# Moving the float64 pieces back by two units, and the packed product's low part forward by one, in a fused attention and MLP kernel

## Chip, cores and metric

The kernel runs on one core of one Trainium2 chip. The metric is device microseconds of one execution. Three runs of the kernel before gave 1552.0, 1552.22 and 1557.69 us, median 1552.22.

## What is computed

The reference, cut to what matters (8 batches, 8 heads, 576 tokens, head size 64, 32 packing queries; 4608 tokens of 512 features go through two MLPs with 1536 and 2048 hidden features):

```
def sm_attn(qq, kk, vv):
    s = scale * np.matmul(qq, kk.transpose(0, 1, 3, 2))
    s = s - np.max(s, axis=-1, keepdims=True)
    a = np.exp(s)
    a = a / (np.sum(a, axis=-1, keepdims=True) + 1e-09)
    return np.matmul(a, vv)
p_packed = sm_attn(p, k, v)
x = sm_attn(q, p_packed, p_packed)          # heads joined to 4608 x 512
x = ((x @ moe_w_a) * (x @ moe_w_b)) @ moe_w_out
h = x @ moe2_w_in
out = (h * np.clip(h + 3.0, 0.0, 6.0) / 6.0) @ moe2_w_out
```

The weights of the MLPs come from the host as float64 words.

## The kernel before

Engines: PE multiplies matrices, PEld loads its weights, DVE, ACT and POOL work on vectors, SP issues the DMAs. Each engine and SP's queue take their instructions in the order in which the program emits them; nothing reorders them later, so the order of the Python calls is the schedule.

Matrices in float32 are multiplied as a high and a low part: `mm3` (L58 to L61) issues three matmuls, high by high, and each high by the other's low. ACT makes a high part by a cast, and DVE or POOL the low part as a difference.

The first MLP is done in four groups of two batches (1152 tokens), each in 12 steps of 128 hidden features: steps 0 to 47, step t belongs to group t // 12. The last matrix of attention, the packed values, is multiplied into the first MLP's weights first. So a step has these parts:

- `pw_unit(t + 1)` (L395): the packed product for the next step, 32 small matmuls (L409) into two of the three PSUM banks named `att`. ACT casts both banks to `pw_hi` (L411). DVE then makes `pw_lo` (L415), which is the last reader of the banks. This subtraction isn't emitted at once: `later(2, rest)` puts it on a list, and `tick()` (L123), called behind each unit of a step and each `y_unit`, counts down and emits what is due.
- four `ab_unit`s (L422), each 12 matmuls of 288 columns, six into each of two tiles in the three `ab` banks. ACT copies the first tile to `a` (L435), DVE multiplies it by the second to `g` (L437), ACT casts `g_hi` (L443), POOL makes `g_lo` (L444).
- `y_unit`s (L452): nine matmuls into one of two `y` banks, then a sum into `acc` on DVE (L464), in the first quarter of a group a copy on ACT (L462). There are 16 for every three steps, emitted between the units as they become ready: in the third step of three, behind the third `ab` unit, first.

The five units of a step come in the order `ab`, `pw`, `ab`, `ab`, `ab`. Behind each unit two slots are filled with background work:

- attention for the next group (`att_units`), whose scores (L176, the tiles `s`) also need two `att` banks at a time,
- in group four, preparation of the second MLP's weights (`w_prep`),
- in groups one to three, **pieces**: 128 x 512 float64 words are rounded to float32. `piece_units` gives five parts for each: two ACT passes (L81, L82) and a DVE shift (L84); a second DVE pass (L88); the store of the piece before (L372); a third DVE pass (L93), which needs ACT's square; POOL's sum (L96), after which the next load is issued. Group one converts the first MLP's weights, groups two and three the second's: 32 pieces, one in a step or two in each third step. Group four has none.

`parts` in the main loop (L711) puts the parts of a step's pieces into slots, two to a unit. In groups two and three they are spread over the first six slots of a step, which begin behind the first `ab` unit, before the packed product.

Behind the first MLP (from about 778 us) the second runs, in six token tiles by eight weight products, with three weight matmuls each as well.

Of the kernel before, what the change touches and what calls it, by code (L numbers as in the profile page):

```python
# [23 lines left out]
NM1 = F1 // P  # L24
# [16 lines left out]
def f32(ap):  # L41
    return ap.bitcast(F32)
# [3 lines left out]
def tile_kernel(ctx: ExitStack, tc: tile.TileContext, qT, kT, vn, pT, wab, wo1, win, wo2, out):  # L46
# [73 lines left out]
    def later(n, fn):  # L120
        due.append([n, fn])
# [19 lines left out]
    def bank(name):  # L141
        tag = banks[n_bank[0] % len(banks)]
        n_bank[0] += 1
        return psum.tile([P, 512], F32, tag=tag, name=name, bufs=BANKS[tag])
# [3 lines left out]
    def lhs_tiles(g):  # L148
        lhs[g] = main.tile([P, 2, 4, NP], F32, tag="lhs", name=f"lhs{g}", bufs=2)
# [130 lines left out]
    def at_split(b, cs=(0, 1)):  # L280
        if b not in at_t:
            at_t[b] = (
                main.tile([P, 2, S], F32R, tag="at_hi", name=f"at_hi{b}", bufs=3),
                main.tile([P, 2, S], F32R, tag="at_lo", name=f"at_lo{b}", bufs=3),
            )
        hi, lo = at_t[b]
        for c in cs:
            a = at32_t.pop((b, c))
            act.copy(hi[:, c, :], a)

            (dve if b == 1 and c == 0 else pool).tensor_sub(lo[:, c, :], a, f32(hi[:, c, :]))  # L291
# [7 lines left out]
    def att_units(b):  # L299

        pk, sf = pack_units(b), soft_units(b)
        lq = [lambda j=j: load_kq(qT, "q", b, j) for j in range(2)]
        ld = loads(b + 1)
        return lq[:1] + pk[:2] + lq[1:] + pk[2:] + ld[:3] + sf[:2] + ld[3:] + sf[2:]
# [13 lines left out]
    def wab_load(t):  # L318

        if NM1 <= t < NSTEP:  # L320
            sp.dma_start(rab_tile(t), wabf[t % NM1])

    def wo_load(t):
        if NM1 <= t < NSTEP:
            m = t % NM1
            sp.dma_start(ro_tile(t), wo1f[m * P:(m + 1) * P, :])
# [68 lines left out]
    def pw_unit(t, wait=2):  # L395

        if t >= NSTEP:
            return
        l = lhs[t // NM1]
        w = rab_t[t].rearrange("p (q n) -> p q n", q=4)  # L400
        hi = main.tile([P, 2, 2, 256], F32R, tag="pw_hi", name=f"pw_hi{t}", bufs=2)
        lo = main.tile([P, 2, 2, 256], F32R, tag="pw_lo", name=f"pw_lo{t}", bufs=2)
        pw_t[t] = (hi, lo)
        ps = [bank(f"pw{t}_{c}").rearrange("p (b n) -> p b n", b=2) for c in range(2)]
        for b in range(2):
            for q in range(4):
                for c in range(2):
                    r, o = slice(64 * c, 64 * c + 64), slice(NP * q, NP * q + NP)
                    pe.matmul(ps[c][o, b, :], lhsT=l[r, b, q, :], rhs=w[r, q, :], start=True, stop=True)  # L409
        for c in range(2):  # L410
            act.copy(hi[:, c], ps[c])  # L411

        def rest():
            for c in range(2):
                dve.tensor_sub(lo[:, c], ps[c], f32(hi[:, c]))  # L415

        if wait:
            later(wait, rest)
        else:
            rest()  # L420
# [112 lines left out]
    def wo_prep(rpool, p):  # L533

        z = {}

        def load():
            z["r"] = rpool.tile([P, 2, CP], F32, tag="raw", name=f"raw_wo{p}")
            for i in range(2):
                sp.dma_start(z["r"][:, i], p2f[2 * p + i, 1])  # L540

        def parts(opool, i):
            hi = opool.tile([P, DM], F32R, tag=f"wo2_hi{p}{i}", name=f"wo2_hi{2 * p + i}")
            lo = opool.tile([P, DM], F32R, tag=f"wo2_lo{p}{i}", name=f"wo2_lo{2 * p + i}")
            wo2_t[2 * p + i] = (hi, lo)
            act.copy(hi, z["r"][:, i])
            pool.tensor_sub(lo, z["r"][:, i], f32(hi))

        return load, parts

    def y_units(pool_, tt):

        z = {}

        def load():
            z["r"] = pool_.tile([P, 4, TP], F32, tag="raw", name=f"raw_y{tt}")
            for k in range(4):
                sp.dma_start(z["r"][:, k], y1d[k, :, tt * TP:(tt + 1) * TP])

        def blk(n):  # L560
            k, j = int(n[1]) - 1, int(n[2]) - 1
            return z["r"][:, 2 * k:2 * k + 2, j * TH:(j + 1) * TH]

        def get(n):
            return blk(n) if n[0] == "B" else z[n]

        def add(to, a, b):
            def fn():
                z[to] = pool_.tile([P, 2, TH], F32, tag="ty", name=f"ty{tt}_{to}", bufs=3)
                pool.tensor_sub(z[to], get(a), get(b))  # L570
            return fn

        def part(n):
            def fn():
                hi = pool_.tile([P, 2, TH], F32R, tag=f"yh{n}", name=f"yh{tt}_{n}")
                lo = pool_.tile([P, 2, TH], F32R, tag=f"yl{n}", name=f"yl{tt}_{n}")
                y_t[n] = (hi, lo)
                act.copy(hi, get(n))
                (pool if n[0] == "B" else dve).tensor_sub(lo, get(n), f32(hi))
            return fn  # L580

        first = [add("T1", "B12", "B11"), add("T2", "B22", "T1"), add("T3", "B22", "B12")]
        t4 = add("T4", "B21", "T2")
        def part4():
            t4()
            part("T4")()
        return load, first, {1: part("B11"), 6: part("T2"), 2: part("B21"), 7: part("T3"), 5: part("T1"), 4: part4, 3: part("B22")}
# [5 lines left out]
    def spread(work, n):  # L593

        return [work[len(work) * i // n:len(work) * (i + 1) // n] for i in range(n)]
# [84 lines left out]
    for t in range(NSTEP):  # L680
        g, m = divmod(t, NM1)
        if m == 0 and g + 1 < NG:
            lhs_tiles(g + 1)
            b = 2 * g + 2
            u0, u1 = att_units(b), att_units(b + 1)
            bg = u0 + u1[:1] + [lambda b=b: at_split(b, (0,))] + u1[1:2] + [lambda b=b: at_split(b, (1,))] + u1[2:]
        if m == 0 and g + 1 == NG:
            sp.dma_start(*stores[-1])
            es_att.close()
            p2a = es_p2a.enter_context(tc.tile_pool(name="p2a", bufs=1, side="right", reuse_waits="tile"))  # L690
            y_load, y_first, y_part = y_units(p2a, 0)
            wo_load0, wo_parts0 = wo_prep(p2a, 0)
            bg = w_prep(p2a, list(range(1, NW)) + [0])
            bg += [y_load, lambda: None, lambda: None] + y_first + [y_part[k] for k in (1, 6, 2, 7, 5, 4, 3)] + [wo_load0]
        wo_load(t + 1)
        left = NM1 - 1 - m
        nb = len(bg) if left == 0 else -(-len(bg) // left)
        todo, bg = spread(bg[:nb], 10), bg[nb:]
        units = [
            (ab_unit, t, 0, 0),  # L700
            (pw_unit, t + 1),
            (ab_unit, t, 0, 1),
            (ab_unit, t, 1, 0),
            (ab_unit, t, 1, 1),
        ]

        if g == 0:
            n_conv = len(by_step[m])
        else:
            n_conv = 2 * NM2 * (t - NM1 + 1) // (2 * NM1) - 2 * NM2 * (t - NM1) // (2 * NM1) if g < 3 else 0  # L710
        parts = spread(list(range(5 * n_conv)), 9 if n_conv > 2 else 6 if g > 0 or n_conv == 2 else 3) + [[]] * 7  # L711
        now = []
        for i, (u, *x) in enumerate(units):
            if (u.__name__[:2], *x) not in ahead:
                u(*x)
            tick()
            if i == 1:
                wab_load(t + 3)
            if g == 0:

                for x in splits.get((t, i), ()):
                    wo_split(*x)
            elif m % SW < 2 and i in (1, 2):
                wo_split(t, i - 1)
            elif m % SW == 1 and i == 4:
                wo_split(t + 1, 0)
            elif m % SW == 2 and i == 1:
                wo_split(t, 1)
            if i in (3, 4) and m == NM1 - 1 and g + 1 < NG:
                at_split(2 * g + 3, (i - 3,))  # L730
            for k in range(2):
                for _ in parts[2 * i + k]:
                    if not now:
                        now = piece_units()
                    now.pop(0)()
                for fn in todo[2 * i + k]:
                    fn()
                if y_ready and (k == 0 or i in (1, 3)) and (y_ready[0][0] * NM1 + y_ready[0][1] * SW + SW - 1, y_ready[0][2] // 2) in wo_t:
                    y_unit(*y_ready.pop(0))
                    tick()  # L740
# [194 lines left out]
```

## Time and profile before

The profile is of one execution, which took 1552.25 us; its span, first to last instruction, is 1550.5 us.

| | PE | PEld | DVE | ACT | POOL |
|---|---|---|---|---|---|
| busy us | 1491.7 | 1347.3 | 872.3 | 682.0 | 491.9 |
| share of the span | 96% | 87% | 56% | 44% | 32% |

Busy is the union of an engine's instructions. Matmuls overlap: one of 288 columns is shown as 0.29 us long, and the next starts 0.13 us after it. Where a row ends in brackets, the number there is the idle time of the engine before it, and behind the arrow stands what ended it. The granted clock of PE is 1.0 of full speed from 150 us on.

### The profile page before, as it was taken

To read this page: it belongs to the slowest core of one execution; us is meant where nothing else is said; L and a number is where in the kernel's file an instruction comes from. 1 tells how busy PE (TensorE), PEld (TensorE's weight loads), DVE (VectorE), ACT (ScalarE), POOL (GpSimd) and SP (SyncE) were. 2 spreads that over 40 slices of the span, in tenths; PEclk is the share of its full clock that TensorE was granted. 3 is DMA by queue.
4 is the path that set the end of the run, shared out by engine and by line. 5 is a ranking of instruction groups with operands and counts; after the bars stand their busy time and mean duration, and the time that the engine had idled before them with its cause. 6 is when DMAs were issued, how large, how long until landed. Compare 5 with 4: busy or idle time off the path is not lost. (4 is left out here: it accounts for less than half of the span.)

```text
span 1550.5 us, 27991 instructions
## 1 busy us (share of the span) xinstructions
PE 1491.7 (96%) x11128; PEld 1347.3 (87%) x11128; DVE 872.3 (56%) x1592; ACT 682.0 (44%) x1453; POOL 491.9 (32%) x483
## 2 busy tenths in 40 slices
PE   4799999999999999999999999999999999999998
PEld 2588898888989899999989988998998998998997
DVE  5778784555754666545544464455455446455443
ACT  4566554554555545554423343343343334234332
POOL 2576653453634545554711130030020021011000
PEclk9799999999999999999999999999999999999999
DMA  8775555655466433664354334344344344333331
GB/s 288 218 220 177 184 191 176 194 160 179 124 198 188 138 125 106 235 219 170 120 180 178 129 141 178 116 162 149 130 152 167 107 172 143 136 144 133 142 138 41
DMA packets 75954, 250.06 MB, mean 161 GB/s; under 512 B 7856, under 2 KB 26288, under 8 KB 68784
## 3 DMA queue, kind: packets, MB, share of 16 engines
q1 hardware_dynamic: 75824, 248.28, 46.6%
q8 instruction: 87, 1.43, 0.4%
q14 instruction: 43, 0.35, 0.1%
HBM read 196.87 MB, written 51.38 MB: 160 GB/s over the span
## 5 line engine op out<-in xcount | busy, mean ns | idle before, releaser
L59 PE MATMUL ab<-at_hi,pw_hi 128*128 128x288 f32 x768 | 234.0, 305 | 8.3 <-ACT a L435 5.5
L61 PE MATMUL ab<-at_hi,pw_lo 128*128 128x288 f32 x768 | 229.1, 298 | 4.3 <-DVE pw_lo L415 4.3
L59 PE MATMUL y<-g_hi,wo_hi 128*128 128x288 f32 x768 | 231.3, 301 | 1.8 <-DVE acc L464 1.7
L60 PE MATMUL ab<-at_lo,pw_hi 128*128 128x288 f32 x768 | 228.6, 298 | 1.2 <-POOL at_lo L291 0.6
L61 PE MATMUL y<-g_hi,wo_lo 128*128 128x288 f32 x768 | 226.4, 295 | 1.0 <-POOL wo_lo L393 1.0
L60 PE MATMUL y<-g_lo,wo_hi 128*128 128x288 f32 x768 | 226.9, 295 | 0.4 <-POOL g_lo L444 0.4
L60 PE MATMUL o<-wo_lo,g2h 128*128 128x512 f32 x576 | 225.0, 391 | 0.0
L61 PE MATMUL o<-wo_hi,g2l 128*128 128x512 f32 x576 | 224.9, 390 | 0.0
L59 PE MATMUL o<-wo_hi,g2h 128*128 128x512 f32 x576 | 224.7, 390 | 0.0
L444 POOL TENSOR_TENSOR g_lo<-g,g_hi 128x288 fp32r<-128x288 f32 x192 | 164.4, 859 | 176.8 <-ACT g_hi L443 172.4
L783 DVE TENSOR_TENSOR g2l<-u,g2h 128x384 fp32r<-128x384 f32 x192 | 121.7, 634 | 140.9 <-ACT g2h L782 136.0
L437 DVE TENSOR_TENSOR g<-a,ab 128x288 f32<-128x288 f32 x192 | 86.4, 451 | 171.7 <-PE ab L61 112.3
L59 PEld LDWEIGHTS ab<-at_hi,pw_hi 128*128 128x128 f32 x768 | 146.6, 191 | 23.7 <-ACT a L435 7.6
L59 PEld LDWEIGHTS y<-g_hi,wo_hi 128*128 128x128 f32 x768 | 144.2, 188 | 19.4 <-DVE acc L464 9.1
L774 ACT ACTIVATE r<-c,half_b 128x384 f32<-128x384 f32 x144 | 88.9, 617 | 144.4 <-DVE c L767 143.9
L61 PEld LDWEIGHTS ab<-at_hi,pw_lo 128*128 128x128 f32 x768 | 146.3, 191 | 4.6 <-DVE pw_lo L415 4.5
L60 PEld LDWEIGHTS ab<-at_lo,pw_hi 128*128 128x128 f32 x768 | 146.5, 191 | 1.7 <-POOL at_lo L291 0.9
L570 POOL TENSOR_TENSOR ty_T<-raw_y 128x768 f32<-128x768 f32 x12 | 23.4, 1952 | 387.1 <-DMA raw_y<-y1d 387.1
L435 ACT COPY a<-ab 128x288 f32<-128x288 f32 x192 | 76.2, 400 | 157.9 <-PE ab L61 156.9
L61 PEld LDWEIGHTS y<-g_hi,wo_lo 128*128 128x128 f32 x768 | 144.3, 188 | 1.5 <-POOL wo_lo L393 1.5
L60 PEld LDWEIGHTS y<-g_lo,wo_hi 128*128 128x128 f32 x768 | 144.3, 188 | 0.6 <-POOL g_lo L444 0.6
L782 ACT CAST g2h<-u 128x384 fp32r<-128x384 f32 x192 | 98.7, 514 | 86.1 <-DVE u L776 84.7
(323 smaller groups left out, 3058.1 us busy)
## 6 DMA issues: line engine op xcount, KB each, us to landing
w<-w2d SPq DMA_DIRECT2D x47, 1792.0 KB, 7.3
rab<-wabf SPq DMA_DIRECT2D x36, 512.0 KB, 5.2
f64p<-in_wo SPq DMA_DIRECT2D x28, 512.0 KB, 3.7
w2d<-w SPq DMA_DIRECT2D x8, 1792.0 KB, 6.7
f64p<-in_wab SPq DMA_DIRECT2D x24, 512.0 KB, 4.6
k<-in_kT SPq DMA_DIRECT2D x16, 576.0 KB, 5.3
q<-in_qT SPq DMA_DIRECT2D x16, 576.0 KB, 5.2
ro<-wo1f SPq DMA_DIRECT2D x36, 256.0 KB, 3.7
```

Source lines behind the costliest of these rows:

```text
L59: pe.matmul(ps, lhsT=l_hi, rhs=r_hi, start=first, stop=False, skip_group_check=skip)
L60: pe.matmul(ps, lhsT=l_hi, rhs=r_lo, start=False, stop=False, skip_group_check=skip)
L61: pe.matmul(ps, lhsT=l_lo, rhs=r_hi, start=False, stop=last, skip_group_check=skip)
L435: act.copy(a, ps[0])
L437: dve.tensor_mul(g32, a, ps[1])
L444: pool.tensor_sub(gl, g32, f32(gh))
L570: pool.tensor_sub(z[to], get(a), get(b))
L774: act.activation(r, c, AF.Relu, bias=half_b, scale=1.0 / 6.0)
L782: act.copy(hi, u)
L783: dve.tensor_sub(lo, u, f32(hi))
```

## The change

Two edits. In `pw_unit` the low part of products for step 12 and later is put on the list with 1, not 2, so that it is emitted by the `tick()` directly behind the product. In the main loop, in groups two to four, four empty slots are put ahead of the pieces' parts: they begin behind the second `ab` unit.

```
-        if wait:
+        if wait and t >= NM1:
+
+            later(1, rest)
+        elif wait:
             later(wait, rest)
         else:
             rest()
...
         parts = spread(list(range(5 * n_conv)), 9 if n_conv > 2 else 6 if g > 0 or n_conv == 2 else 3) + [[]] * 7
+        if g > 0:
+
+            parts = [[]] * 4 + parts
```

PE's instructions stand in the same order before and after. On the other engines the order is another from step 11 on, and from there lines are numbered 3 higher. The first place is DVE in step 17, around the low part of the product for step 18. The names: `g_17_0` is the product for step 17's first `ab` unit, `cv_ap` a piece, `pw_lo` the low part. Before:

```order
L437 TENSOR_TENSOR g_17_0_4531<-a_0_4529,ab_01_4522 128x288
L84 TENSOR_SCALAR cv_ap_0_4541<-f64p_0_3905 128x512
L88 SCALAR_TENSOR_TENSOR cv_ap_0_4541<-f64p_0_3905,cv_ap_0_4541 128x512
L93 SCALAR_TENSOR_TENSOR cv_ap_0_4541<-cv_sqp_0_4538,cv_ap_0_4541 128x512
L84 TENSOR_SCALAR cv_ap_1_4585<-f64p_1_3943 128x512
L437 TENSOR_TENSOR g_17_1_4607<-a_1_4605,ab_11_4598 128x288
L415 TENSOR_TENSOR pw_lo_4548<-pw_0_4549,pw_hi_4547 128x512
L415 TENSOR_TENSOR pw_lo_4548<-pw_1_4550,pw_hi_4547 128x512
```

The same place in the changed kernel:

```order
L440 TENSOR_TENSOR g_17_0_4531<-a_0_4529,ab_01_4522 128x288
L415 TENSOR_TENSOR pw_lo_4540<-pw_0_4541,pw_hi_4539 128x512
L415 TENSOR_TENSOR pw_lo_4540<-pw_1_4542,pw_hi_4539 128x512
L440 TENSOR_TENSOR g_17_1_4591<-a_1_4589,ab_11_4582 128x288
L84 TENSOR_SCALAR cv_ap_0_4599<-f64p_0_3953 128x512
L88 SCALAR_TENSOR_TENSOR cv_ap_0_4599<-f64p_0_3953,cv_ap_0_4599 128x512
L440 TENSOR_TENSOR g_17_2_4633<-a_2_4631,ab_21_4624 128x288
L93 SCALAR_TENSOR_TENSOR cv_ap_0_4599<-cv_sqp_0_4596,cv_ap_0_4599 128x512
```

The low part has moved ahead of four passes of pieces and of `g_17_1`.

The second place is ACT in step 14, from the cast of the product for step 15 to the copy of the third `ab` unit. `cv_sqp` and `p2f` are a piece's two passes, `a_1` and `a_2` the copies of the second and third `ab` unit. Before:

```order
L81 ACTIVATE cv_sqp_0_3863<-f64p_0_2971 128x512
L82 ACTIVATE p2f_0_3862<-f64p_0_2971 128x512
L236 COPY lhs_3297<-bd_3870 128x128
L411 CAST pw_hi_3873<-pw_0_3875 128x512
L411 CAST pw_hi_3873<-pw_1_3876 128x512
L443 CAST g_hi_0_3858<-g_14_0_3856 128x288
L392 CAST wo_hi_3899<-ro_3555 128x256
L81 ACTIVATE cv_sqp_1_3908<-f64p_1_3176 128x512
L82 ACTIVATE p2f_1_3907<-f64p_1_3176 128x512
L435 COPY a_1_3929<-ab_10_3915 128x288
L435 COPY a_2_3959<-ab_20_3945 128x288
```

In the changed kernel:

```order
L236 COPY lhs_3297<-bd_3862 128x128
L411 CAST pw_hi_3865<-pw_0_3867 128x512
L411 CAST pw_hi_3865<-pw_1_3868 128x512
L446 CAST g_hi_0_3858<-g_14_0_3856 128x288
L392 CAST wo_hi_3893<-ro_3555 128x256
L438 COPY a_1_3913<-ab_10_3899 128x288
L81 ACTIVATE cv_sqp_0_3920<-f64p_0_2971 128x512
L82 ACTIVATE p2f_0_3919<-f64p_0_2971 128x512
L438 COPY a_2_3943<-ab_20_3929 128x288
```

The first piece has moved from before the product's cast to behind `a_1`, the second to a place after these rows.

The third place is POOL at the border of groups three and four. `p2f` are the sums of the last two pieces, `at_lo` is the attention output's low part, and `raw_w` the first weight sums of group four, which follow these rows. Before:

```order
L96 TENSOR_TENSOR p2f_0_8670<-cv_ap_0_8674,p2f_0_8670 128x512
L96 TENSOR_TENSOR p2f_1_8710<-cv_ap_1_8714,p2f_1_8710 128x512
L444 TENSOR_TENSOR g_lo_1_8735<-g_35_1_8732,g_hi_1_8734 128x288
L291 TENSOR_TENSOR at_lo_8765<-at_8607,at_hi_8764 128x576
L444 TENSOR_TENSOR g_lo_2_8761<-g_35_2_8758,g_hi_2_8760 128x288
L291 TENSOR_TENSOR at_lo_8765<-at_8644,at_hi_8764 128x576
L444 TENSOR_TENSOR g_lo_3_8813<-g_35_3_8810,g_hi_3_8812 128x288
L444 TENSOR_TENSOR g_lo_0_8856<-g_36_0_8853,g_hi_0_8855 128x288
```

In the changed kernel:

```order
L447 TENSOR_TENSOR g_lo_1_8721<-g_35_1_8718,g_hi_1_8720 128x288
L291 TENSOR_TENSOR at_lo_8753<-at_8605,at_hi_8752 128x576
L96 TENSOR_TENSOR p2f_0_8722<-cv_ap_0_8726,p2f_0_8722 128x512
L447 TENSOR_TENSOR g_lo_2_8749<-g_35_2_8746,g_hi_2_8748 128x288
L291 TENSOR_TENSOR at_lo_8753<-at_8644,at_hi_8752 128x576
L447 TENSOR_TENSOR g_lo_3_8809<-g_35_3_8806,g_hi_3_8808 128x288
L96 TENSOR_TENSOR p2f_1_8772<-cv_ap_1_8776,p2f_1_8772 128x512
L447 TENSOR_TENSOR g_lo_0_8856<-g_36_0_8853,g_hi_0_8855 128x288
```

The last piece's sum now stands behind all low parts of step 35; its store, and on SP's queue the loads for `raw_w` behind it, follow that sum.

## Rows read from the trace of the kernel before

**Rows 1.** The page, busy us by engine: share of the span, instructions.

```profile
PE 1491.7 (96%) x11128; PEld 1347.3 (87%) x11128; DVE 872.3 (56%) x1592; ACT 682.0 (44%) x1453; POOL 491.9 (32%) x483
```

**Rows 2.** Stretches: us, then busy PE, PEld, DVE, ACT, POOL; PEclk, DMA, GB/s.

```profile
224.00:612.00 388.00, 377.15 (x3819) 343.97 (x3825) 230.64 (x454) 198.06 (x471) 185.76 (x202) 1.00 0.49 156
612.00:778.00 166.00, 165.12 (x1489) 156.58 (x1480) 82.33 (x153) 81.58 (x195) 95.66 (x112) 1.00 0.53 187
```

**Rows 3.** Waits of PE, 224 to 612 us: us in total, times, longest us.

```profile
PE s L176 <- DVE pw_lo L415: 4.0, 3, 2.7
PE ab L59 <- ACT a L435: 3.5, 5, 0.7
PE y L59 <- DVE acc L464: 1.7, 2, 1.3
PE pv L226 <- ACT et L215: 0.6, 2, 0.3
PE y L60 <- POOL g_lo L444: 0.4, 1, 0.4
```

**Rows 4.** Waits of PE, 612 to 778 us.

```profile
PE ab L59 <- ACT a L435: 0.4, 1, 0.4
PE ab L59 <- DVE g L437: 0.4, 1, 0.4
```

**Rows 5.** Timeline of PE, a stopped and a free block: start us, us, instruction.

```profile
320.03 0.67 PE L176 MATMUL s<-k,p 64*32 64x288 f32 x2
323.38 0.71 PE L176 MATMUL s<-k,p 64*32 64x288 f32 x14 [2.69 <-DVE pw_lo L415]
324.03 0.40 PE L59 MATMUL ab<-at_hi,pw_hi 128*128 128x288 f32 x1
...
331.00 0.71 PE L176 MATMUL s<-k,p 64*32 64x288 f32 x16
331.65 0.40 PE L59 MATMUL ab<-at_hi,pw_hi 128*128 128x288 f32 x1
```

**Rows 6.** Timeline of ACT and DVE, step 17, ahead of that block.

```profile
318.40 1.07 ACT L411 CAST pw_hi<-pw 128x512 fp32r<-128x512 f32 x2
...
322.18 0.45 DVE L437 TENSOR_TENSOR g<-a,ab 128x288 f32<-128x288 f32 x1 [1.21 <-ACT a L435]
322.55 1.28 DVE L415 TENSOR_TENSOR pw_lo<-pw,pw_hi 128x512 fp32r<-128x512 f32 x2
```

**Rows 7.** Timeline of PE and ACT, step 14.

```profile
276.11 0.29 PE L61 MATMUL ab<-at_hi,pw_lo 128*128 128x288 f32 x1
277.12 0.40 PE L59 MATMUL ab<-at_hi,pw_hi 128*128 128x288 f32 x1 [0.72 <-ACT a L435]
...
275.24 0.42 ACT L392 CAST wo_hi<-ro 128x256 fp32r<-128x256 f32 x1
...
276.67 0.70 ACT L435 COPY a<-ab 128x288 f32<-128x288 f32 x2
```

**Rows 8.** Timeline of ACT and PE, group four, step 38, the same place.

```profile
644.14 0.41 ACT L435 COPY a<-ab 128x288 f32<-128x288 f32 x1
...
644.75 0.30 PE L61 MATMUL ab<-at_hi,pw_lo 128*128 128x288 f32 x1
644.88 0.29 PE L59 MATMUL ab<-at_hi,pw_hi 128*128 128x288 f32 x1
```

**Rows 9.** Timeline of POOL and DVE, two passes that overlap.

```profile
309.26 1.16 POOL L271 TENSOR_TENSOR t<-t,sm 128x576 f32<-128x576 f32 x1 [0.97 <-DVE sm L270]
...
309.45 1.51 DVE L93 SCALAR_TENSOR_TENSOR cv_ap<-cv_sqp,cv_ap 128x512 f32<-128x512 f32 x1
```

**Rows 10.** Groups by line, 224 to 612 us: count, busy us, mean ns, idle before.

```profile
L81 ACT ACTIVATE cv_sqp<-f64p 128x512 f32<-128x512 f32 x33 | 22.7, 688 | 0.0
...
L93 DVE SCALAR_TENSOR_TENSOR cv_ap<-cv_sqp,cv_ap 128x512 f32<-128x512 f32 x33 | 26.3, 798 | 0.9
```

**Rows 11.** Timeline of POOL, the first weight sum of group four.

```profile
617.84 0.73 POOL L509 TENSOR_TENSOR raw_w<-raw_w 128x256 f32<-128x256 f32 x1 [2.60 <-DMA raw_w<-p2f]
```

## What the change should do

> **What bounds the kernel now.** First the page's busy times: PE, the matrix engine, works 96% of the span of 1550.5 us, the next engine 56% [rows 1]. So time can come only out of PE's idle time, and it has to be looked for where the change acts. That is from 224 us, just before the packed product for the first step of group two is made, to the end of group four. The table by stretches [rows 2] cuts this at 612 us, in the first step of group four: up to there PE is busy 377.15 of 388.00 us, so 10.85 idle; after it 165.12 of 166.00, so 0.88. Then PE's waits in the first stretch, sorted by who ended them [rows 3]: 4.0 us for the packed product's low part (three times, once 2.7), 3.5 for the copy `a` of a first-MLP result (five times, each 0.7), 1.7 for an `acc` sum, 0.6 for `et`, 0.4 for a `g_lo`. Together 10.2 of the 10.85. In group four, where no piece is converted and no attention runs, two waits remain, 0.8 us [rows 4].
>
> **What the change moves, and what stays.** The order of PE's instructions is the same before and after, so the 377.15 busy us stay. No work is added or removed: a piece is two ACT passes of 0.69 (33 of them, one of which closes group one), three DVE passes (the last 0.80 on average), one POOL sum and two DMAs [rows 10]. What can change is only when these stand in front of something PE waits for. Group four converts nothing, so there only the low part moves, and no wait of [rows 4] is for it: I cost it at nothing.
>
> **The low part.** The attention scores (L176) need two of the three `att` banks, and the product holds two until DVE has made its low part. In step 17 the scores begin at 320.03, two matmuls run, the next waits 2.69, and the block is left only at 324.03: 4.00 us; an undisturbed block of 16 takes 0.65, from 331.00 to the next matmul at 331.65 [rows 5]. So this wait costs 3.35, of which the list counts 2.69 as idle: a stop costs 0.66 more than its idle time in such a block. The other two share 4.0 - 2.7 = 1.3 idle, so 0.65 + 0.65 = 1.3 each: 5.95 in all. Why so late: ACT had both halves of `pw_hi` done at 319.47, yet DVE started the low part at 322.55, because before it stood the piece's passes and a product `g` that waited for `a` [rows 6]. In the new order DVE goes from `g_17_0` straight to the low part. Two halves of `pw_hi` take 1.07 together and two of the low part 1.28 [rows 6], so, with a little overlap, some 0.59 and 0.68 each. The first half of the low part can start when the first of `pw_hi` is done, 318.40 + 0.59 = 318.99, and 0.68 later the first bank is free: 319.7, before the scores want it at 320.1. In the other two one `y` unit of nine matmuls, 1.2 us, lies between product and scores, about what `pw_hi` and `pw_lo` need after it, so I leave 0.2 us for each. Gain 5.6; bounds 0 (another holder of the bank) and 5.95.
>
> **The pieces.** The five waits for `a` stand in five of the eight steps with two pieces, those where the product is followed by two `ab` units and no `y`. At step 14 the stream of matmuls breaks from 276.11 to 277.12 [rows 7], 1.01 us where 0.13 is regular (644.75 to 644.88 [rows 8]): 0.88, of which 0.72 idle. ACT shows why: the cast before ends at 275.66, then the second piece's two passes run, and `a` comes at 276.67. In the new order they stand behind `a`, which would run from about 275.55 to 275.95, ahead of the 276.24 at which PE wants it. Group four has the same place without a piece: there `a` ends at 644.55 and PE passes at 644.88 without a stop. Five times 0.88 is 4.4; I take 4.2, bounds 0 and 4.4. Two waits for `et` (0.6) have the first piece's passes before the copies on ACT, and these go too: 0.6. The 0.65 that is left of the 10.85 I leave as it is. The `acc` and `g_lo` waits (2.1 idle in three stops, and 0.16 for each to refill the stream, as 0.88 - 0.72 says) come almost all in step 29, where softmax passes and both pieces crowd DVE in its first units; in the new order the sums stand before part of the pieces: 2.0 of 2.6, bounds 0 and 2.6.
>
> **What is queued behind what.** On DVE the low part now stands before the `acc` sums and can make them wait for `pw_hi`. At 318.31 + 0.1 + 0.59 + 2 x 0.68 it would be done 2.0 us after the product's end, a sum 0.45 later; PE comes back to that `y` bank after two `y` units and an `ab` unit, 1.2 + 1.2 + 1.6 = 4.0 us at 0.13 a matmul. Cover 1.5 us. On ACT the piece's 1.3 us now stands before the copy of the third `ab` unit; the bank is wanted one `ab` tile, two `y` and one tile later, 0.8 + 2.4 + 0.8 = 4.0 us. On POOL the last sum of a piece comes later, behind `g_lo`. On SP the loads of the next pieces wait until a piece's DVE pass has freed their buffer, and will do so later in the step; behind them stand `rab`, used three steps on, and `ro`, used one step on, of some 15.5 us (388 for 25 steps): nothing. At the boundary the last piece ends a few us later, and POOL's first weight sum of group four, which waited 2.60 us for its load [rows 11], will wait longer; behind it stand `g_lo` tiles that PE needs two steps later. Nothing again, but that is a bound from one row. For new waits as a whole the nearest row is group four, where weight preparation of like size stands in the same late units: 0.8 us in 166, so 1.9 in 388. I take 1.9, bounds 0 and the 10.85 that the stretch holds now.
>
> **Sum.** 5.6 + 4.2 + 0.6 + 2.0 = 12.4 gained, 1.9 given back: 10.5. The profiled execution took 1552.25 us, the median of the runs is 1552.22, so they can be set equal: 1552.25 - 10.5 = 1541.75, say **1541.5 us**. About 0.5% (7.8 us: 1544.5 and 1560.0) is what a measurement of this kernel can tell from no change.
>
> **Rivals.** (1) *The waits move on.* With its early stops gone PE runs ahead, and the one-piece steps, 16 in groups two and three, meet a late `a` or `acc` in their last units. For it: nearly all of the 4.0 us covers assume that ACT and DVE are on time. Against: over these 388 us neither is loaded to 60% [rows 2]. At 0.5 us a step, one short stop as above, 8 us: 1541.5 + 8 = 1549.5; at half that 1545.5. Chance 0.21, nearly all within 0.5%. (2) *DVE becomes the bound: slower.* A piece's pass can take 1.51 us instead of its usual 0.7 beside a POOL pass that started just before [rows 9], and pieces now meet the `g_lo` passes and the `acc` sums of the crowded units. It decides once DVE is behind by more than the 2.8 us that one `y` and one `ab` unit give. The `acc` and `g_lo` stops of one step cost 2.6 above; if the eight two-piece steps each lost that and the 16 others 0.5: 20.8 + 8 - 12.4 = 16.4 slower, 1568.7. Against: DVE has 157 of 388 us free. Chance 0.05. The Trainium skill, "SBUF — State Buffer", section "SBUF: two separate sides", says that a DVE pass with two SBUF inputs and a POOL pass exclude each other for a whole instruction. The 1.51 agrees with it. (3) *Much faster.* PE's weight loads are busy 343.97 of 388, 88.7%, but 94.3% in group four; at that share the stretch would take 364.7, 23 less: 1529. Against: the stretch holds attention matmuls with small weights that keep their spacing, and its idle time is 10.85 only. Chance 0.02. The Trainium skill, "Perfetto Trace Analysis", section "Identifying the Most-Contended Engine", judges headroom by that share and not by busy matmuls. (4) *It does nothing:* `pw_hi` or another bank holder ends the waits just as late, 1552. Step 17, where `pw_hi` was done 3 us before the low part began, speaks against it. Chance 0.04. The forecast keeps 0.68.
>
> **Numbers.** Faster by over 0.5%: 0.68 + 0.02 = 0.70. Within: 0.21 + 0.04 = 0.25. Slower: 0.05. The range goes down to 1537 (10.85 idle and about 4 of refilling all gone, 14.9) and up to 1549, into rival 1; outside lie rivals 2 to 4 and the end of 1, some 0.15.
>
> **What would show it.** In the profile after: PE's waits up to about 600 us name no `pw_lo` for L176; `a` is gone or once; idle of the stretch near 3 us where 10.85 stood; group four shorter by nothing. A low part that still starts 3 us after its `pw_hi` would refute the first term, a copy `a` that still follows a piece's passes the second, new waits for `acc` or `a` in the one-piece steps would be rival 1, and DVE passes of pieces mostly over 1 us rival 2. If the time falls although these waits stand, my reading is wrong altogether.

## The result and the profile after

The changed kernel takes **1540.98 us** (median of 4 runs, 1538.78 to 1543.84); the kernel before, on the same chip, 1552.37 (1552.0 to 1557.69, 4 runs). The ratio is 0.9909, with a 95% interval of 0.9889 to 0.9930: faster, by 0.7 to 1.1%. The profiled execution took 1538.86 us with a span of 1537.1, 13.4 less than before. Executions of one kernel differ by 5 to 6 us among themselves, so below a stretch of one profile measures an edit better than a time does.

The page of the changed kernel, busy us by engine, stands against [rows 1]: PE's share rose from 96 to 97%, with the same 11128 instructions.

```profile
PE 1485.1 (97%) x11128; PEld 1344.4 (87%) x11128; DVE 875.8 (57%) x1592; ACT 680.5 (44%) x1453; POOL 495.7 (32%) x483
```

The table by stretches of the changed kernel, cut at the same places of the program as [rows 2], just before product 12, just behind the start of product 37, and at the same distance behind product 47 (us, busy PE, PEld, DVE, ACT, POOL; PEclk, DMA, GB/s):

```profile
223.28:597.71 374.43, 373.07 (x3819) 343.43 (x3825) 232.45 (x454) 196.70 (x471) 186.63 (x201) 1.00 0.48 161
597.71:763.95 166.24, 164.93 (x1488) 156.38 (x1478) 83.67 (x153) 81.68 (x195) 97.96 (x113) 1.00 0.53 188
```

The first stretch is 13.57 us shorter. PE's idle time in it fell from 10.85 to 1.36 us, by 9.49, and its busy time from 377.15 to 373.07, by 4.08, though its 3819 instructions are the same: a matmul right behind a stop is shown as 0.40 us, one in a running stream as 0.29 [rows 7, 8], so part of what a stop costs stands in the busy time. PE's waits of the changed kernel from 224 to 602 us, against [rows 3]:

```profile
PE y L59 <- ACT wo_hi L392: 0.7, 1, 0.7
PE y L61 <- POOL wo_lo L393: 0.3, 1, 0.3
PE y L60 <- POOL g_lo L447: 0.2, 1, 0.2
PE pw L409 <- ACT ex L189: 0.2, 1, 0.2
```

Neither `pw_lo`, `a`, `acc` nor `et` is left. One wait is new: `wo_hi`, 0.7.

**Where it came from.** On PE's timeline the distance from the start of one packed product (L409) to the start of the next is a clean measure, because PE's order never changes: from product 7 on, where nothing differs, the two kernels agree within 0.02 us (but for 0.24 behind product 45, see the end of the section on the prediction). From product 12 (at 224 us) to product 37 the kernel before takes 387.61 us, the changed one 374.03: **13.58 less**. From 37 to 47 it is 142.29 and 142.53, before product 12 187.01 and 186.88, so all of it lies in groups two and three. The distances that differ, in us, worked out from the starts in PE's timeline of each kernel (the last three columns are experiments below):

| behind product | before | after | pieces alone | low part alone | one unit |
|---|---|---|---|---|---|
| 12 | 13.13 | 13.84 | 13.12 | 13.84 | 13.82 |
| 13 | 18.92 | 17.74 | 18.92 | 17.73 | 17.74 |
| 15 | 15.03 | 14.03 | 14.31 | 15.01 | 14.99 |
| 18 | 17.40 | 14.02 | 17.82 | 14.76 | 14.78 |
| 21 | 15.00 | 14.04 | 14.05 | 14.99 | 15.00 |
| 24 | 13.32 | 12.35 | 12.92 | 13.32 | 13.33 |
| 25 | 18.95 | 17.76 | 18.95 | 17.76 | 17.77 |
| 27 | 14.13 | 13.71 | 13.71 | 15.26 | 15.20 |
| 28 | 18.41 | 17.74 | 17.74 | 18.40 | 17.74 |
| 30 | 16.01 | 13.63 | 13.64 | 16.14 | 13.82 |
| 31 | 17.72 | 17.53 | 17.50 | 17.73 | 17.53 |
| 33 | 15.79 | 15.40 | 15.39 | 16.94 | 16.88 |
| 34 | 16.53 | 15.92 | 15.93 | 16.74 | 15.92 |
| 35 | 13.55 | 13.55 | 13.54 | 14.02 | 13.54 |
| 36 | 13.30 | 12.34 | 12.93 | 13.30 | 13.34 |
| 12 to 37 | 387.61 | 374.03 | 380.86 | 386.38 | 381.80 |

The timelines of the changed kernel show how. First step 17, against [rows 5, 6]:

```profile
317.84 0.71 PE L176 MATMUL s<-k,p 64*32 64x288 f32 x16
318.49 0.40 PE L59 MATMUL ab<-at_hi,pw_hi 128*128 128x288 f32 x1
...
316.21 1.08 ACT L411 CAST pw_hi<-pw 128x512 fp32r<-128x512 f32 x2 [1.08 <-PE pw L409]
...
316.83 1.29 DVE L415 TENSOR_TENSOR pw_lo<-pw,pw_hi 128x512 fp32r<-128x512 f32 x2 [0.93 <-ACT pw_hi L411]
318.89 0.46 DVE L440 TENSOR_TENSOR g<-a,ab 128x288 f32<-128x288 f32 x1 [0.77 <-ACT a L438]
319.26 1.63 DVE L84 TENSOR_SCALAR cv_ap<-f64p 128x512 uint32<-128x512 uint32 x1
```

ACT casts as soon as the product is there, DVE stands idle for `pw_hi` and starts the low part 0.62 us behind it, where it started 4.15 behind before (318.40 and 322.55). The score block runs in one piece, 0.65 us. The piece's first pass comes behind it and takes 1.63, off PE's path. Then step 14, against [rows 7]:

```profile
274.31 0.41 ACT L438 COPY a<-ab 128x288 f32<-128x288 f32 x1
274.60 0.70 ACT L81 ACTIVATE cv_sqp<-f64p 128x512 f32<-128x512 f32 x1
275.17 0.68 ACT L82 ACTIVATE p2f<-f64p 128x512 int32<-128x512 uint16 x1
275.73 0.41 ACT L438 COPY a<-ab 128x288 f32<-128x288 f32 x1
...
274.92 0.30 PE L61 MATMUL ab<-at_hi,pw_lo 128*128 128x288 f32 x1
275.05 0.29 PE L59 MATMUL ab<-at_hi,pw_hi 128*128 128x288 f32 x1
```

The copy `a` stands ahead of the piece's two passes, ends at 274.72, 0.33 before PE passes from one `ab` unit to the next, and PE goes on at its 0.13.

The new wait stands at the border of groups one and two. DVE, ACT and PE of the changed kernel:

```profile
225.44 1.28 DVE L415 TENSOR_TENSOR pw_lo<-pw,pw_hi 128x512 fp32r<-128x512 f32 x2
226.64 0.91 DVE L93 SCALAR_TENSOR_TENSOR cv_ap<-cv_sqp,cv_ap 128x512 f32<-128x512 f32 x1
...
227.68 1.29 POOL L96 TENSOR_TENSOR ro<-cv_ap,ro 128x512 int32<-128x512 int32 x1 [0.68 <-POOL g_lo L447]
...
229.00 0.40 ACT L392 CAST wo_hi<-ro 128x256 fp32r<-128x256 f32 x1 [2.59 <-POOL ro L96]
...
229.46 0.40 PE L59 MATMUL y<-g_hi,wo_hi 128*128 128x288 f32 x1 [0.68 <-ACT wo_hi L392]
```

The low part for step 12, emitted one unit earlier, now stands ahead of the last pass of group one's last piece; POOL's sum, ACT's cast and PE follow one behind the other. Price: 13.84 against 13.13, 0.71.

### The profile page after: what moved, and what is told of

It is laid out like the page before. It is cut to its first block, busy times and chain, and to the rows that moved or that the text cites. A ratio compares the mean times of both kernels' runs of the same rounds, so it can differ in the third digit from the quotient of the medians.

```text
span 1537.1 us, 27977 instructions
## 1 busy us (share of the span) xinstructions
PE 1485.1 (97%) x11128; PEld 1344.4 (87%) x11128; DVE 875.8 (57%) x1592; ACT 680.5 (44%) x1453; POOL 495.7 (32%) x483
## 5 line engine op out<-in xcount | busy, mean ns | idle before, releaser
L447 POOL TENSOR_TENSOR g_lo<-g,g_hi 128x288 fp32r<-128x288 f32 x192 | 167.5, 874 | 169.1 <-ACT g_hi L446 167.1
```

The source lines that it names most:

```text
L447: pool.tensor_sub(gl, g32, f32(gh))
```

## Experiments

Each kernel is the changed one with the edit shown; "stretch" is product 12 to product 37.

**The pieces alone.** The low part goes back to two units behind.

```
-        if wait and t >= NM1:
-            later(1, rest)
-        elif wait:
+        if wait:
             later(wait, rest)
```

> The pieces begin four slots later as in the changed kernel, the low part stays two units behind the product. Theory (each wait goes with the instruction that stood in front of it): no wait for the copy a and none for et in groups two to four, no acc wait in step 29; but the attention scores (L176) still wait three times for pw_lo, because the low part stands behind acc_01 in steps 12 and 24 (0.65 us idle each, as before) and behind g_17_1 in step 17 (about 2 us where 2.69 stood). Idle of PE in the stretch from step 11 to step 36 about 4.5 us (10.85 before, 1.4 with both edits), gain in that stretch about 9 of 13.6 us, time near 1543.5. Rival (either edit gives the early units enough room, and the waits share one cause): no pw_lo wait over 0.3 us, stretch idle under 2.5, time 1540 to 1542.

Measured: 1546.31 us (1545.48 to 1550.16, 6 runs), ratio to before 0.9953 [0.9935, 0.9971]; stretch 380.86, 6.75 less than before. The first two of PE's waits, 224 to 612 us:

```profile
PE s L176 <- DVE pw_lo L415: 2.9, 3, 1.6
PE y L59 <- DVE acc L464: 0.6, 2, 0.3
```

The waits for `a` and `et` are gone, those for `pw_lo` are not: which edit removes which is as expected. The gain is smaller than the 9 us expected, for two reasons. The first was not foreseen: the `acc` wait of 1.3 in step 29 is gone, but two of 0.3 stand behind products 24 and 36, and the distances behind 15, 24 and 36 stay 0.28, 0.57 and 0.59 above those of the changed kernel. The second is that the distance behind product 18 is even longer than before (17.82 and 17.40), though the stop in it is shorter (1.6 and 2.7). That is the clock, below.

**The low part alone.**

```
-            parts = [[]] * 4 + parts
+            parts = parts
```

> The low part comes one unit behind the product as in the changed kernel, the pieces stay where they were before. Theory: no wait of the scores for pw_lo; the five waits for a (0.7 us each), the two for et (0.3 each) and the acc wait in step 29 (about 1.3) stay, and the wait of y for wo_hi at the border of groups one and two (0.68 us) is there as with both edits. Stretch idle about 6.5 us, gain about 6 us, time near 1546.5; the gains of the two single edits add up to that of both within 1.5 us. Rival (one shared cause): a waits gone or halved too, stretch idle under 4, time under 1543.

Measured: 1553.75 us (1551.28 to 1554.77, 12 runs), ratio 0.9987 [0.9976, 0.9997]; stretch 386.38, only 1.23 less than before, where about 6 was expected. PE's waits, 224 to 612 us:

```profile
PE ab L59 <- ACT a L438: 3.9, 6, 0.7
PE y L59 <- DVE acc L467: 2.2, 3, 1.5
PE bd L234 <- DVE pp L230: 1.9, 2, 1.0
PE y L59 <- ACT wo_hi L392: 0.7, 1, 0.7
```

No `pw_lo` any more, and the products 13, 18 and 25 gain 1.19 + 2.64 + 1.19 = 5.02. But a sixth wait for `a` (in step 17, part of what 18 falls short), the border's 0.71, and losses at 27, 30, 33, 34 and 35 take 1.13 + 0.13 + 1.15 + 0.21 + 0.47 + 0.71 = 3.80 back. The largest two are a wait that neither kernel has, for `pp`. DVE and PE of this kernel behind product 27:

```profile
458.61 1.27 DVE L415 TENSOR_TENSOR pw_lo<-pw,pw_hi 128x512 fp32r<-128x512 f32 x2
459.79 0.92 DVE L93 SCALAR_TENSOR_TENSOR cv_ap<-cv_sqp,cv_ap 128x512 f32<-128x512 f32 x1
460.64 0.95 DVE L84 TENSOR_SCALAR cv_ap<-f64p 128x512 uint32<-128x512 uint32 x1
461.51 0.46 DVE L230 TENSOR_SCALAR pp<-pv,rs 128x64 f32<-128x64 f32 x2
...
462.12 0.30 PE L234 MATMUL bd<-ident,pp 128*128 128x128 f32 x1 [0.97 <-DVE pp L230]
```

and DVE of the changed kernel at the same place:

```profile
451.34 1.29 DVE L415 TENSOR_TENSOR pw_lo<-pw,pw_hi 128x512 fp32r<-128x512 f32 x2 [1.07 <-ACT pw_hi L411]
452.54 0.47 DVE L230 TENSOR_SCALAR pp<-pv,rs 128x64 f32<-128x64 f32 x2
```

The low part now stands ahead of two passes of pieces, 1.7 us, and `pp` comes behind all three. Where the pieces begin later, none of their passes stands between the low part and `pp`. So the low part's edit is worth little without the other.

**All low parts early but two.** This takes exactly that wait away from the low part alone.

```
-        if wait and t >= NM1:
+        if wait and t >= NM1 and t not in (27, 33):
...
-            parts = [[]] * 4 + parts
+            parts = parts
```

> The low part alone one unit behind the product, the pieces where they were before, but the products for steps 27 and 33 keep two units: their steps hold the attention value product, and with the low part alone PE waited there 0.97 us each for pp. Theory (what the low part alone gave back is the low part standing on DVE before pp, together with a piece's two passes): no wait of bd for pp, the steps behind products 27 and 33 fall from 15.26 and 16.95 us to the 14.13 and 15.80 of the kernel before, the stretch to product 37 from 386.4 to about 384.1 us. Rival (the lost time comes from something else that the low part alone does, such as more POOL collisions): those two steps stay over 15 and 16.5.

Measured: 1550.73 us (1548.26 to 1553.73, 10 runs), ratio 0.9968 [0.9955, 0.9981]; stretch 384.10, 2.28 less than with the low part alone. The `pp` waits are gone, the distances behind 27 and 33 are 14.12 and 15.80 as before, and the other waits stay (`a` 4.0 in six). The reading holds.

**One unit.** Two empty slots in place of four.

```
-            parts = [[]] * 4 + parts
+            parts = [[]] * 2 + parts
```

> Both edits, but the pieces are put back by two slots (one unit) only, so the first piece's two ACT passes stand between the product's cast and the copy a_1. Theory (what counts is a piece's pass between the cast and a): five waits of PE for a of about 0.7 us come back, 3.5 us idle, no pw_lo wait; time 1541.0 + 4.4 = near 1545.4. Rival (what counted was the load of two pieces on ACT ahead of a, of which only one is left): a waits under 1 us in all, time within 1 us of 1541.

Measured: 1549.58 us (1546.8 to 1552.51, 11 runs), ratio 0.9966 [0.9952, 0.9979]; stretch 381.80, 7.77 more than the changed kernel. PE's waits, 224 to 612 us, then ACT and PE in step 14:

```profile
PE ab L59 <- ACT a L438: 3.9, 6, 0.7
PE bd L234 <- DVE pp L230: 2.6, 2, 1.3
```

```profile
274.95 0.69 ACT L81 ACTIVATE cv_sqp<-f64p 128x512 f32<-128x512 f32 x1
275.52 0.68 ACT L82 ACTIVATE p2f<-f64p 128x512 int32<-128x512 uint16 x1
276.08 0.40 ACT L438 COPY a<-ab 128x288 f32<-128x288 f32 x1
...
276.54 0.40 PE L59 MATMUL ab<-at_hi,pw_hi 128*128 128x288 f32 x1 [0.69 <-ACT a L438]
```

The piece is again ahead of `a`, as in [rows 7], and the stop of 0.69 is back. So it is the copy's place behind the piece, not the piece's work, that costs. The `pp` wait I had not foreseen; it is the one of the low part alone. Of the 7.77, 15, 21, 24, 36 and 18 (`a`) make 4.66 and 27 and 33 (`pp`) 2.97.

**Crowded.** The pieces start behind seven empty slots, where the changed kernel has four, and stand closer, to see whether DVE or ACT can become the bound.

```
-            parts = [[]] * 4 + parts
+            parts = [[]] * 7 + spread(list(range(5 * n_conv)), 3)
```

> As the changed kernel, but the pieces' parts are put into the last three slots of the step only. Theory (PE returns to a y bank or an ab bank some 4 us after it left it, so a late copy or sum is covered): one-piece steps lose nothing; two-piece steps, where six DVE passes and four ACT passes now stand between the last y sums and the next step's first copy, lose up to 0.5 us each; the stretch to product 37 grows from 374.0 to between 374 and 378 us, time 1541 to 1545. Rival (DVE or ACT becomes the bound once pieces are dense): two-piece steps lose 2 us and more, the stretch takes over 385 us, time over 1552.

Measured: 1544.82 us (1543.23 to 1545.06, 4 runs), ratio 0.9927 [0.9907, 0.9946]; stretch 377.06, 3.03 more than the changed kernel. PE's waits, 224 to 612 us:

```profile
PE s L176 <- DVE pw_lo L415: 0.7, 1, 0.7
PE y L59 <- ACT wo_hi L392: 0.7, 1, 0.7
PE pw L409 <- ACT ex L189: 0.6, 1, 0.6
PE y L60 <- POOL g_lo L447: 0.5, 1, 0.5
```

Against the changed kernel `pw_lo` is new, `ex` and `g_lo` have grown, and a wait of 0.4 for `g` follows in the list; the loss lies mostly behind products 25, 30 and 31 (1.25, 0.93, 0.49). The total is as expected, its place is not: 25 and 31 are made in steps 24 and 30, which have one piece and come right behind steps with two, and most steps with two lost nothing. It is a cost, but far from the 16 us of rival 2, and still faster than before.

**The border.** The product for step 12 keeps its low part two units behind.

```
-        if wait and t >= NM1:
+        if wait and t > NM1:
```

> As the changed kernel, but the low part of the product for step 12 keeps its place two units behind, so that the last piece of group one isn't held up on DVE by it. Theory: the wait of y for wo_hi at about 229.5 us falls from 0.68 us to under 0.2, the steps from 13 on stand 0.7 us earlier relative to step 12, time 0.7 us lower, about 1540.3, too little to be told by the times. Rival (that wait is scatter between executions): it stays over 0.5.

Measured: 1541.03 us (1538.61 to 1541.28, 5 runs), ratio 0.9907 [0.9890, 0.9924]. The wait for `wo_hi` is gone, the distance behind product 12 is 13.13 again, the stretch 373.36, 0.67 less than the changed kernel. That is the best version of the stretch; the times cannot tell it from the changed kernel.

**The border and step 6.** In group one the score block of step 6 still waits 0.8 us for `pw_lo`; this kernel emits that low part early too.

```
-        if wait and t >= NM1:
+        if wait and (t > NM1 or t == 6):
```

> As the run before with the border mended, and in group one the low part of the product for step 6 also comes one unit behind it; attention scores follow that product, and the wait for pw_lo there (0.81 us idle near 134 us, about 1.7 us with what the block loses beside it) should go. Theory: the time between the products for steps 6 and 7 falls by 1.5 to 1.7 us, nothing else moves by over 0.1; time about 1.6 under the run with the border mended, near 1539. Rival (group one's pieces, which the low part now passes on DVE, feed the same group's weights and make PE wait instead, as at the border): under 0.5 us won, a wait for rab, wo_hi or wo_lo appears between 130 and 165 us.

Measured: 1540.28 us (1538.22 to 1540.9, 5 runs), ratio 0.9896 [0.9878, 0.9913]; the stretch is 373.35. PE's waits of this kernel from 100 to 224 us:

```profile
PE pw L409 <- POOL rab L96: 2.3, 2, 1.8
PE y L61 <- POOL wo_lo L393: 1.2, 1, 1.2
```

`pw_lo` is not among them, but a wait for `wo_lo` of 1.2 has come, and the distance behind product 6 is 19.44 (19.42 in the changed kernel; 19.87 in the profile of the border kernel, where the stop for `pw_lo` was 1.2 and not 0.8): the wait moved on, and at most 0.4 us was won, as the rival said.

**Two profiles more: the clock.** To see why the pieces alone gained less than expected, it and the kernel before were profiled once more, unchanged.

> The same kernel as pieces_alone, profiled a second time. In the first profile the granted clock of TensorE went to half from about 321.6 to 325.0 us, right behind the stop for the low part in step 17, and the interval behind product 18 was 17.82 us, where the stop alone (1.58 idle + 0.66 over 14.02) would give 16.26. Theory A: the half clock belongs to this stop in this order of instructions: it shows again, interval 17.8, stretch from product 12 to 37 near 380.9. Rival B: it is scatter between executions: the clock stays full there, interval near 16.3, stretch near 379.3, and the half clock may show at another stop or nowhere.

> The kernel before, profiled a second time. Theory A (the clock follows the order of instructions): as in the first profile no half clock between 224 and 612 us, interval behind product 18 17.40, stretch 387.6. Rival B (scatter): a half clock of 3 us or so behind the longest stop, 2.69 us in step 17, interval 18 near 19.0, stretch near 389.2.

Measured: the pieces alone 1546.51 us, distance behind product 18 17.80 (17.82 in its first profile). The kernel before 1556.55 us, where its first profile had 1552.25; all its waits of [rows 3] are the same to 0.1 us, yet behind product 18 it needs 18.94, not 17.40. The stretches of the pieces alone (first profile) and of the kernel before (second profile), columns as above; the number ahead of the DMA share is the granted clock:

```profile
320.00:322.00 2.00, 0.64 (x14) 0.21 (x14) 1.84 (x4) 1.19 (x3) 1.85 (x2) 0.90 0.18 70
322.00:324.00 2.00, 2.00 (x14) 1.67 (x8) 0.84 (x2) 0.70 (x2) 0.00 (x0) 0.50 0.30 16
324.00:326.00 2.00, 2.00 (x13) 2.00 (x13) 0.47 (x2) 0.73 (x2) 0.81 (x1) 0.74 0.62 231
```

```profile
324.00:326.00 2.00, 0.12 (x7) 0.15 (x14) 1.32 (x3) 0.59 (x2) 2.00 (x3) 1.00 0.29 117
326.00:328.00 2.00, 2.00 (x20) 1.53 (x17) 1.88 (x3) 0.70 (x2) 0.64 (x1) 0.64 0.35 131
328.00:330.00 2.00, 2.00 (x10) 2.00 (x9) 0.09 (x1) 0.73 (x2) 1.96 (x2) 0.51 0.82 243
```

And PE behind the stop in the kernel before, second profile, where [rows 5] shows the first:

```profile
325.88 0.71 PE L176 MATMUL s<-k,p 64*32 64x288 f32 x14 [2.70 <-DVE pw_lo L415]
326.52 0.61 PE L59 MATMUL ab<-at_hi,pw_hi 128*128 128x288 f32 x1
326.93 0.44 PE L60 MATMUL ab<-at_lo,pw_hi 128*128 128x288 f32 x1
327.17 0.44 PE L61 MATMUL ab<-at_hi,pw_lo 128*128 128x288 f32 x1
```

Right behind the stop for the low part in step 17, TensorE's granted clock was at 0.50, its lower level of 1.2 GHz, for some 3 us, and a matmul came every 0.24 us, not 0.13. It cost 18.94 - 17.40 = 1.54 us in the kernel before, and 17.82 - (14.02 + 1.58 + 0.66) = 1.56 in the pieces alone, where 0.66 is what a stop costs beyond its idle time. For the pieces alone theory A held (the half clock came again), for the kernel before rival B (in one of two profiles). None of the kernels without that stop has a stretch under full clock from 224 us to the end of group four.

## Why the prediction was right

The mechanism is right: both edits removed the waits they were meant to remove, for the reasons given. The time, 1541.5 against 1540.98, is right too, but that it is right to 0.5 us is luck. The changed kernel's four runs took 1538.78, 1538.86, 1543.1 and 1543.84, and their median falls where none of them lies; the medians are 11.4 apart. Against the base of the forecast, the profiled execution, the gain was 13.4 where 10.5 was forecast: 1.2 of the difference are terms sized a little too small, 0.67 a stop that no term named, 1.19 new waits that did not come.

One statement of the prediction is wrong: that PE's busy time stays and time can come only out of its idle time. Between the same instructions 4.08 of the 13.57 came out of busy time. The sum did not suffer, because each stop was priced with its refilling, which is most of what the busy time lost, and the lower end of the range names it ("about 4 of refilling").

- **The low part: right, 5.6 forecast.** Products 13, 18 and 25 gained 1.18 + 3.38 + 1.19 = 5.75, so the two that I left at 0.2 short each went fully. The 0.66 that a stop in a score block costs on top of its idle time is borne out. A fourth such stop, 0.67 behind product 28, does not stand in the list of waits: there ACT cast `pw_hi` behind a piece, and a block of 16 scores took 1.45 us (474.75 to 476.20), 0.78 in the changed kernel. It goes with the pieces' edit, as the table shows. And one thing was missing from the term: in some executions the stop of 2.7 us is followed by 3 us of half clock, another 1.54 that the change takes away.
- **`a`: right, 4.2 forecast.** 15, 21, 24 and 36 gained 1.00 + 0.96 + 0.97 + 0.96, a little over the 0.88 a stop; the fifth lies in 30. One unit brings them back: the cause is shown.
- **`et`: right,** 0.81 at 27 and 33 (0.6 forecast). **`acc` and `g_lo`: right in kind,** 30, 31 and 34 gained 2.38 + 0.19 + 0.61, with one `a` (0.9) in it some 2.3 against 2.0.
- **New waits: the step that was mis-sized.** "I take 1.9" of group four's rate was a price for waits all along the stretch; the trace has one, 0.71, at a place that I had not named: the border of groups one and two, where the low part passes group one's last piece. My list of what is queued behind what covered `acc`, `a`, `g_lo` and the loads, and not the last pass of a piece whose `ro` sum the next step's weights wait for. 5.75 + 0.67 + 3.89 + 0.81 + 3.18 - 0.71 = 13.59, the whole of the stretch.
- **Rival 1** did not come: between products 12 and 37 the distance grew behind 12 alone. **Rival 2:** its lengthening is real. The piece's first pass (L84) took 804 ns on average where it took 697, once 1.63 us beside POOL's `at_lo` (319.15 to 320.60), off PE's path. The Trainium skill, "SBUF — State Buffer", section "SBUF: two separate sides", lets a DVE pass and a POOL pass exclude each other where the DVE pass has two SBUF inputs or works in a mode that takes two ports; by its row this pass has one input tile, so it would be the second, which no run here shows. Even the crowded kernel lost 3 us, not 16 or more. **Rival 3**, which judged by weight loads (91.7% of the stretch now, against 88.7%), is refuted as a size: once the idle time is gone, the time does not fall on. **Rival 4** is refuted by the low part's rows of step 17.
- The border of groups three and four cost nothing, as forecast. POOL's first weight sum of group four waited longer for its load, and PE did not wait for it. POOL of the changed kernel, against [rows 11]:

```profile
606.09 0.74 POOL L512 TENSOR_TENSOR raw_w<-raw_w 128x256 f32<-128x256 f32 x1 [5.14 <-DMA raw_w<-p2f]
```

One thing that the prediction took for granted fell: that each edit's gain is its own. The low part alone gives 1.23 and the pieces alone 6.75, or 8.3 without the half clock; together 9.5 of 13.58. The other 4.0 us come only when both are made.

Open: the kernel before's two levels of time, 1552.25 and 1556.55, are accounted for (2.47 between products 0 and 12, 189.48 against 187.01, 1.54 behind product 18, 0.24 behind product 45: 4.25 of 4.30). Of the 2.47, 2.05 lie before product 6, where half-clock spells before 80 us stand at other places, and 0.44 behind product 6, where the stop for `pw_lo` was 1.18 and not 0.77. All eleven profiles show one or the other: 186.87 to 187.06 us between products 0 and 12 in six, 188.85 to 189.54 in the five that have a half-clock spell at 60 to 64 us. What sets that, and the two levels of the changed kernel's times, was not settled.

## What to carry to other kernels

Sum PE's waits in the stretch that an edit touches and price each stop by the distance it opens in the stream, which is its idle time plus what refilling costs (0.16 in a long stream, 0.66 in a block of small matmuls); that gave 12.4 here, and the chip gave 14.3, of which the one new wait took 0.7 back. In an in-order queue, whatever moves forward pushes something else back: for every step moved, name the instruction now behind it and who waits for that, at the borders of loops above all, and don't expect two such edits to add up or to work apart.

## What was not expected of the hardware

A stop of PE can cost twice. Three of the four profiles that have the stop in step 17 (1.6 to 2.7 us idle) show TensorE at its lower level for some 3 us right behind it, at a price of 1.5 us; the fourth, the first of the kernel before, shows full clock behind 2.69 us. The other two stops for the low part in the pieces alone, 0.64 us each, left the clock at 1.00. A stop that neither edit touches shows it more often: behind product 6, in group one, PE waits 1.79 to 1.81 us for `rab`, and in all eleven profiles the granted clock is at 0.50 for 3 to 4 us from at most 1.6 us behind that stop. The stop of 1.33 to 1.69 us for `a` near 86 us is followed by a granted clock of 1.00 in all eleven. What decides between the two was not settled.
